# Half-wide operations where the second layer runs alone, and its input parts made a slot later

## The chip, the cores and the metric

The kernel runs on one core of one Trainium2 chip. The metric is the device time of an execution in microseconds. The engines are named as the profile names them: PE (TensorE, matrix products), PEld (its weight loads), DVE (VectorE), ACT (ScalarE), POOL (GpSimd) and SP (SyncE, which here only issues transfers).

## The reference

An attention with pooled keys feeds two layers in a row, each a product, a pointwise function and a second product. All tensors are float32, there are 12288 tokens of width 128, and each layer has 2048 hidden columns.

```
kv_pool = kv averaged over 4 x 4 patches          # 768 keys of width 128
k = v = kv_pool @ w_sr
a = softmax(q @ k.T / sqrt(128));  x1 = a @ v

h = x1 @ w_in1;  g = h * clip(h + 3, 0, 6) / 6;  x2 = g @ w_out1
h = x2 @ w_in2;  g = h if h >= 1, 0 if h <= -1, else (h + 1)^2 / 4
out = g @ w_out2
```

## The kernel before, in words

**Work and staging.** Tokens go in 24 blocks (`NB`) of 512, hidden columns in 8 pairs of 128 (`NPAIR`), so a layer has 192 steps `s` (`NS`): step s is pair s mod 8 of block s // 8. A float32 product is made as three products of a high and a low part (high by high, high weight by low input, low weight by high input). So `m_in(m, s)` (L461) is six products of 512 columns, three into each of two PSUM banks that form one tile `h` of 128x1024; two such tiles are in use, taken in turn. `m_out(m, s)` (L473) is six products that add into the one bank `acc[m]`, over the 8 steps of a block. m is 0 for the first layer and 1 for the second.

**Between the products** of the second layer a step goes through four engines' queues: `clip2` (L530, DVE, from the bank), `sq2` (L539, ACT), `max2` (L543, DVE, which is the last to read the bank), then `hi_lo` (L548): the high part is a copy on ACT (L555), the low part a subtraction on POOL (L556), on DVE only where s is 191. The first layer has `relu1` (L518, ACT), `mul1` (L523, DVE) and `hi_lo`. All of them work on 128x1024 at once, except where `parts` (L510) gives two halves of 128x512: from slot 20 on that is only s = 191 of either layer.

**Order.** The program is written out by hand: each engine runs its instructions in the order in which the loop over slots T (L743) issues them. Slot T takes step T of the first layer and step T - 11 (`O2`) of the second. Slots 0 to 19 are `early_slot` (L612), where a step has two separate banks; the others are `slot` (L650). There PE's order is `m_in(0, T)`, `m_out(1, ..)` by `out2` (L606), `m_in(1, T - 11)`, products of the attention in some slots, `m_out(0, T - 1)`. `out2` takes the step that is 13 slots behind, from slot 197 on 14 behind, so slot 197 has no `m_out(1, ..)`. From T = 192 on the first layer has nothing left but `m_out(0, 191)`, and the second layer runs alone, to slot 205; the same function `slot` issues that with conditions on T:

```
m_in(1, s2); clip2(s2); sq2(s2)
max2(s2 - 1); hi_lo(1, s2 - 1)
m_out(0, 191)        # slot 192 alone
out2(T)
```

**The input of the second layer.** When `m_out(0, s)` has ended a block, which is at the end of each slot T with T mod 8 = 0, it issues two instructions that make the high part `x2h` (L493, ACT) and the low part `x2l` (L494, DVE) from `acc[0]`. They are first needed three slots later, by `m_in(1, ..)`; `acc[0]` is written again by the `m_out(0, ..)` at the end of the next slot.

Of the kernel before, what the change touches and what calls it, by code (L numbers as in the profile page):

```python
# [9 lines left out]
F32R = mybir.dt.float32r  # L10
# [5 lines left out]
ALU = mybir.AluOpType  # L16
# [3 lines left out]
O2, LAG2 = 11, 2  # L20
# [20 lines left out]
JOIN_T = 20  # L41
# [5 lines left out]
def tile_attn_moe_moe2(  # L47
# [14 lines left out]
    nc = tc.nc  # L62
# [3 lines left out]
    BLK = 512  # L66
# [39 lines left out]
    def f32(t):  # L106
        return t.bitcast(FP32)
# [288 lines left out]
    def s_exp(b, j):  # L396
        e, su, s, ps, nm = e_t[b, j]
        if j == 3:
            qT_t.pop(b)
        if s is None:  # L400
            s2 = sm_p.tile([128, 2], FP32, tag="s2", name="s2")
            for h in range(2):
                nc.scalar.activation(
                    out=e[:, h * 384:(h + 1) * 384], in_=ps[h], func=ACTF.Exp, bias=nm, scale=1.0,
                    accum_out=s2[:, h:h + 1],
                )
            nc.vector.tensor_tensor(out=su, in0=s2[:, 0:1], in1=s2[:, 1:2], op=ALU.add)
        else:
            nc.scalar.activation(
                out=e.rearrange("p (a b) -> p a b", a=2), in_=s[:, :, :384], func=ACTF.Exp, bias=nm,  # L410
                scale=1.0, accum_out=su,
            )
# [48 lines left out]
    def m_in(m, s):  # L461
        b, c = divmod(s, NPAIR)
        assert (m, "in", c // 2) in ready
        hi, lo = (x_t, x2_t)[m][b]
        wh, wl = w_in[m]
        h_t[m, s] = new_pair() if paired(m, s) else [new_h(), new_h()]
        for k in range(2):
            ps = h_t[m, s][:, k] if paired(m, s) else h_t[m, s][k]
            ws = slice((2 * c + k) * 128, (2 * c + k + 1) * 128)
            for n, (l, r) in enumerate(((wh, hi), (wh, lo), (wl, hi))):  # L470
                nc.tensor.matmul(ps, l[:, ws], r, start=(n == 0), stop=(n == 2))  # L471

    def m_out(m, s):  # L473
        b, c = divmod(s, NPAIR)
        assert (m, "out", c // 2) in ready
        if c == 0:
            acc[m] = ps_a.tile([128, BLK], FP32, tag=f"acc{m}", name=f"acc{m}")
        hi, lo = hl_t.pop((m, s))
        wh, wl = w_out[m]
        order = [(k, n) for k in range(2) for n in range(3)]  # L480
        if (m, s) == (1, NS - 1):
            order = [(0, 0), (0, 2), (1, 0), (1, 2), (0, 1), (1, 1)]
        for i, (k, n) in enumerate(order):
            ws = slice((2 * c + k) * 128, (2 * c + k + 1) * 128)
            l, r = ((wh, hi), (wh, lo), (wl, hi))[n]
            nc.tensor.matmul(  # L486
                acc[m], l[:, ws], r[:, k, :], start=(c == 0 and i == 0), stop=(c == NPAIR - 1 and i == 5)
            )
        if c == NPAIR - 1:
            if m == 0:  # L490
                hi = x_p.tile([128, BLK], F32R, tag="x2h", name="x2h")
                lo = x_p.tile([128, BLK], F32R, tag="x2l", name="x2l")
                nc.scalar.copy(out=hi, in_=acc[0])  # L493
                nc.vector.tensor_tensor(out=lo, in0=acc[0], in1=f32(hi), op=ALU.subtract)  # L494
                x2_t[b] = (hi, lo)
            else:
                o_t[b] = acc[1]

    def o_T(b):
        o = o_p.tile([128, BLK], FP32, tag="o", name="o")  # L500
# [9 lines left out]
    def parts(m, s, h=None):  # L510
        h = h if h is not None else g_t[m, s]
        if not paired(m, s):
            return [(k, h[k] if isinstance(h, list) else h[:, k]) for k in range(2)]
        if s == NS - 1:
            return [(k, h[:, k]) for k in range(2)]
        return [(slice(0, 2), h)]

# [45 lines left out]
    def ok(s):  # L563
        return 0 <= s < NS
# [47 lines left out]
    def early_slot(T):  # L612
        s1, s2 = T, T - O2
        if ok(s1):
            m_in(0, s1)
            relu1(s1)
        if T in tail_at:
            s_tail_a(*tail_at[T], on_act=T < ACT_T)
        mul1(s1)
        if ok(s2):  # L620
            m_in(1, s2)
            clip2(s2)
        if ok(s2 - 1):
            hi_lo(1, s2 - 1)
        hi_lo(0, s1)
        if ok(s2):
            sq2(s2)
        if T in s_at:
            s_mm(*s_at[T])
        if T in tail_at:  # L630
            s_tail_b(*tail_at[T])
        if ok(s2):
            max2(s2)
        if T in s_at:
            s_exp(*s_at[T])
        if T in av_at:
            av(*av_at[T], early=T < O2)
        if T in q_at:
            q_T(q_at[T])
        conv_step(T in CONV_AT)  # L640
        load_next()
        if ok(s1 - 1):
            m_out(0, s1 - 1)
        if T in o_at:
            o_T(o_at[T])
        out2(T)
# [2 lines left out]

    def slot(T):  # L650
        s1, s2 = T, T - O2
        if ok(s1):
            m_in(0, s1)
        if ok(s2 - 1) and JOIN_T < T < NS:
            max2(s2 - 1)
        if T in tail_at and T > JOIN_T:
            s_exp(*tail_at[T])
        if ok(s1):
            relu1(s1)
        if ok(s2 - 1) and T < NS:  # L660
            hi_lo(1, s2 - 1)
        if T in tail_at:
            s_tail_a(*tail_at[T])
        if T < NS:
            out2(T)
        if ok(s1):
            mul1(s1)
        if T in o_at and T < NS:
            o_T(o_at[T])
        if ok(s2):  # L670
            m_in(1, s2)
        if ok(s1):
            hi_lo(0, s1)
        if ok(s2):
            clip2(s2)
        if ok(s2):
            sq2(s2)
        if ok(s2 - 1) and T >= NS:
            max2(s2 - 1)
            hi_lo(1, s2 - 1)  # L680
        if T in tail_at:
            s_tail_b(*tail_at[T])
        if T in s_at:
            s_mm(*s_at[T])
        if T in av_at:
            av(*av_at[T])
        if T in q_at:
            q_T(q_at[T])
        if ok(s1 - 1):
            m_out(0, s1 - 1)  # L690
        if T >= NS:
            out2(T)
            if T in o_at:
                o_T(o_at[T])

    with tc.manual_schedule():
        load_next()
        nc.scalar.dma_start(out=wsr, in_=w_sr)
        make_identity(nc, ident)
        nc.vector.tensor_reduce(  # L700
            out=pool_m.rearrange("p (a q) -> p a q", a=4),
            in_=ident.rearrange("p (a r q) -> p a q r", a=4, r=4), axis=AX.X, op=ALU.add,
        )
        nc.vector.tensor_scalar(out=pool_m, in0=pool_m, scalar1=1.0 / 16.0, scalar2=None, op0=ALU.mult)
        mem = {}

        def v_stat():
            mem["mxa"] = v_scale()

        def v_sv():  # L710
            mem["sv"] = v_split(mem["mxa"])

        def q_step(b):
            q_T(b)
            q_done.add(b)

        steps = {f"k{i}": (lambda i=i: kv_pool(i)) for i in range(NG // 2)}
        steps |= {f"g{i}": (lambda i=i: kv_sum_mm(i)) for i in range(NG // 2)}
        for m in range(KC):
            steps[f"t{m}"] = lambda m=m: kv_poolT(m)  # L720
            steps[f"p{m}"] = lambda m=m: k_mm(m)
            steps[f"z{m}"] = lambda m=m: k_split(m)
            steps[f"y{m}"] = lambda m=m: v_max(m)
        for n in range(len(w_jobs)):
            for st in range(4):
                steps[f"j{n}.{st}"] = lambda n=n, st=st: conv_stage(n, st)
        for j in range(4):
            steps[f"s{j}"] = lambda j=j: s_mm0(0, j, j in SPLIT0)
            steps[f"S{j}"] = lambda j=j: s_half(0, j, 1)
            steps[f"n{j}"] = lambda j=j: s_max(0, j, 0)  # L730
            steps[f"N{j}"] = lambda j=j: s_max(0, j, 1)
            steps[f"e{j}"] = lambda j=j: s_exp(0, j)
            steps[f"a{j}"] = lambda j=j: s_tail_a(0, j, True)
            steps[f"b{j}"] = lambda j=j: s_tail_b(0, j)
        steps |= {
            "vm": v_stat, "vs": v_sv, "vh": lambda: v_hi(mem["sv"]), "vl": lambda: v_lo(mem["sv"]),
            "q0": lambda: q_step(0), "q1": lambda: q_step(1),
            "x0": lambda: av(0, 0, True), "x1": lambda: av(0, 1, True),
        }
        for name in PROLOGUE.split():  # L740
            steps[name]()
            load_next()
        for T in range(NS + O2 + 16):  # L743
            if T == JOIN_T:
                join_banks()
            (early_slot if T < JOIN_T else slot)(T)


# [28 lines left out]
```

## Time and profile before

| what | value |
|---|---|
| median of 3 runs | 1387.58 us (1385.89 to 1390.67) |
| the profiled execution, its own time | 1386.09 us |
| its span, first to last instruction | 1384.3 us |
| PE busy | 1322.7 us, 96% of the span |
| DVE busy | 1104.6 us, 80% |
| POOL busy | 1057.2 us, 76% |
| ACT busy | 968.3 us, 70% |

The 1.8 us between the span and the profiled execution's time lie outside the first and last instruction. Busy shares are means over stages that differ: the first 200 us (keys, weights, early slots), a long middle, and the end from slot 192 on.

### The profile page before, as it was taken

What the parts mean: (1) busy time and instruction counts of PE and PEld (TensorE: products, weight loads), DVE (VectorE), ACT (ScalarE), POOL (GpSimd) and SP (SyncE); (2) the same over time, 40 slices, a digit from 0 to 9 for tenths busy, and PEclk for the clock granted to TensorE, in tenths of its full rate; (3) what the DMA queues carried; (4) which work ended last, traced back from release to release, by engine and by line L of the source; (5) the groups of instructions that cost most, each with busy time, mean ns of one, the idle gap of its engine ahead of it and who ended that gap; (6) DMA issues with size and microseconds to landing.
All of it is one profiled execution on the core that took longest, in us unless ns stands there. A gap on an engine that the chain in (4) does not pass through costs nothing.

```text
span 1384.3 us, 17050 instructions
## 1 busy us (share of the span) xinstructions
PE 1322.7 (96%) x6244; PEld 1070.6 (77%) x6244; DVE 1104.6 (80%) x1286; ACT 968.3 (70%) x1205; POOL 1057.2 (76%) x473
## 2 busy tenths in 40 slices
PE   8587999999999999999999999999999999999975
PEld 7465778888888888888888888888888888888754
DVE  3798978887887887888888888888878878877665
ACT  2677877767776776776777677677677767766753
POOL 2488988887887877787787787788877878778854
PEclk9799999999999999999999999999999999999999
DMA  9542121221221221221221212212212211211000
GB/s 320 135 83 50 46 50 31 42 43 35 46 38 35 39 50 35 39 50 27 47 42 31 50 31 42 51 31 42 45 34 45 39 35 31 42 35 20 8 3 14
DMA packets 260772, 66.20 MB, mean 48 GB/s; under 512 B 252368, under 2 KB 256592, under 8 KB 260688
## 3 DMA queue, kind: packets, MB, share of 16 engines
q1 hardware_dynamic: 259456, 62.94, 22.8%
q10 hardware_dynamic: 1232, 2.16, 0.4%
q8 instruction: 50, 0.82, 0.2%
q14 instruction: 34, 0.28, 0.1%
HBM read 21.04 MB, written 6.29 MB: 20 GB/s over the span
## 4 chain that ended last, share of the span: by engine, by line
PE 83%; DVE 7%; ACT 2%; POOL 2%; issue 2%; DMA 0%; POOLq 0%; DVEq 0%; ACTq 0%
PE h L471 36%; PE acc L486 35%; PE s L373 6%; PE s L445 6%; POOL l L556 1%; DVE g L535 1%; DVE g L546 1%; DVE a L430 1%; ACT h L555 1%; DVE t L526 1%; DVE nm L384 1%; DVE wa L181 0%; ACT t L521 0%; DVE t L535 0%; DVE t L546 0%
## 5 line engine op out<-in xcount | busy, mean ns | idle before, releaser
L556 POOL TENSOR_TENSOR l<-g,h 128x1024 fp32r<-128x1024 f32 (+1 forms) x195 | 451.0, 2315 | 249.4 <-issue 200.3
L556 POOL TENSOR_TENSOR l<-t,h 128x1024 fp32r<-128x1024 f32 (+1 forms) x216 | 540.8, 2507 | 20.9 <-ACT h L555 15.2
L526 DVE SCALAR_TENSOR_TENSOR t<-t,h 128x1024 f32<-128x1024 f32 (+1 forms) x213 | 235.1, 1111 | 94.0 <-ACT t L521 93.7
L521 ACT ACTIVATE t<-h 128x1024 f32<-128x1024 f32 (+1 forms) x213 | 198.9, 942 | 135.9 <-PE h L471 90.7
L535 DVE TENSOR_SCALAR g<-h 128x1024 f32<-128x1024 f32 (+1 forms) x195 | 227.8, 1172 | 67.7 <-PE h L471 65.0
L541 ACT ACTIVATE g<-g 128x1024 f32<-128x1024 f32 (+1 forms) x195 | 198.4, 1021 | 114.9 <-DVE g L535 111.7
L555 ACT CAST h<-t 128x1024 fp32r<-128x1024 f32 (+1 forms) x220 | 210.7, 965 | 84.9 <-DVE t L526 82.8
L546 DVE TENSOR_TENSOR g<-h,g 128x1024 f32<-128x1024 f32 (+1 forms) x195 | 226.2, 1164 | 21.2 <-ACT g L541 21.1
L555 ACT CAST h<-g 128x1024 fp32r<-128x1024 f32 (+1 forms) x195 | 194.9, 1005 | 6.1 <-DVE g L546 5.4
L471 PE MATMUL h<-x2h,wi1h 128*128 128x512 f32 x384 | 155.1, 404 | 12.8 <-DVE g L546 6.8
L471 PE MATMUL h<-xh,wi0h 128*128 128x512 f32 x384 | 152.9, 398 | 7.7 <-ACT xh L450 5.0
L486 PE MATMUL acc<-l,wo1h 128*128 128x512 f32 x384 | 152.1, 397 | 8.3 <-POOL l L556 8.3
L486 PE MATMUL acc<-h,wo0h 128*128 128x512 f32 x384 | 156.3, 407 | 0.0
L486 PE MATMUL acc<-l,wo0h 128*128 128x512 f32 x384 | 153.1, 399 | 2.3 <-POOL l L556 2.1
L471 PE MATMUL h<-xl,wi0h 128*128 128x512 f32 x384 | 152.5, 397 | 0.7 <-DVE xl L451 0.7
L471 PE MATMUL h<-x2h,wi1l 128*128 128x512 f32 x384 | 152.2, 396 | 0.0
L486 PE MATMUL acc<-h,wo0l 128*128 128x512 f32 x384 | 152.2, 396 | 0.0
L471 PE MATMUL h<-xh,wi0l 128*128 128x512 f32 x384 | 152.1, 396 | 0.0
L486 PE MATMUL acc<-h,wo1h 128*128 128x512 f32 x384 | 151.6, 395 | 0.3 <-ACT h L555 0.3
L471 PE MATMUL h<-x2l,wi1h 128*128 128x512 f32 x384 | 151.7, 395 | 0.0
L486 PE MATMUL acc<-h,wo1l 128*128 128x512 f32 x384 | 151.4, 394 | 0.0
L430 DVE SCALAR_TENSOR_TENSOR a<-e,rc,a 128x768 f16<-128x768 f32 x96 | 133.5, 1390 | 0.6 <-ACT a L423 0.5
(136 smaller groups left out, 2122.2 us busy)
## 6 DMA issues: line engine op xcount, KB each, us to landing
q<-in_q_dram SPq DMA_DIRECT2D x96, 64.0 KB, 2.3
out_dram<-o SPq DMA_DIRECT2D x96, 64.0 KB, 1.9
h<-in_kv_dram SPq DMA_DIRECT2D x4, 512.0 KB, 8.8
l<-in_moe_w_in_dram SPq DMA_DIRECT2D x3, 512.0 KB, 9.1
at<-a SPq DMA_TRANSPOSE x96, 3.7
g<-in_moe_w_in_dram SPq DMA_DIRECT2D x2, 512.0 KB, 6.6
h<-in_moe_w_out_dram SPq DMA_DIRECT2D x2, 512.0 KB, 9.3
l<-in_kv_dram ACTq DMA_DIRECT2D x2, 512.0 KB, 10.5
```

The lines of the kernel that those rows point to most:

```text
L373: nc.tensor.matmul(ps[h], l[:, js], r[:, ks], start=(n == 0), stop=(n == 2))
L430: nc.vector.scalar_tensor_tensor(out=a[:, 1], in0=e, scalar=rc, in1=a[:, 0], op0=ALU.mult, op1=ALU.subtract)
L445: nc.tensor.matmul(ps, l[:, k, :], r[:, k, :], start=(n == 0), stop=(n == 3 * KC - 1))
L471: nc.tensor.matmul(ps, l[:, ws], r, start=(n == 0), stop=(n == 2))
L486: nc.tensor.matmul(acc[m], l[:, ws], r[:, k, :], start=(c == 0 and i == 0), stop=(c == NPAIR - 1 and i == 5))
L521: nc.scalar.activation(out=g[:, p], in_=h, func=ACTF.Relu, scale=1.0 / 6.0, bias=0.5)
L526: nc.vector.scalar_tensor_tensor(out=g[:, p], in0=g[:, p], scalar=1.0, in1=h, op0=ALU.min, op1=ALU.mult)
L535: nc.vector.tensor_scalar(out=g[:, p], in0=h, scalar1=1.0, scalar2=-1.0, op0=ALU.min, op1=ALU.max)
L541: nc.scalar.activation(out=g, in_=g, func=ACTF.Square, scale=0.5, bias=0.5)
L546: nc.vector.tensor_tensor(out=g[:, p], in0=h, in1=g[:, p], op=ALU.max)
L555: nc.scalar.copy(out=hi[:, p], in_=g)
L556: eng.tensor_tensor(out=lo[:, p], in0=g, in1=f32(hi[:, p]), op=ALU.subtract)
```

## The change

The two instructions that make `x2h` and `x2l` leave `m_out` and become a function `x2_parts`. In early slots it stands where it stood. In `slot(T)` it is called with T - 1, behind `mul1` of slot T: so the parts of a block are made in the slot after the one that ended the block, on ACT behind `relu1` and the copy of `hi_lo(1, ..)`, on DVE behind `max2`, the start of a softmax tail and `mul1`. For the last block it comes in slot 193.

The slots from 192 on get a function of their own, `last_slot`. In it `max2(s2)` follows `sq2(s2)` in the same slot, `hi_lo(1, s2 - 1)` stands between `clip2(s2)` and `sq2(s2)`, and `max2` of step 180 comes first of all. `parts` now gives two halves for the second layer's steps 181 to 191, which are those that `last_slot` starts, so `clip2`, `sq2`, `max2` and `hi_lo` of these steps are two half-wide instructions each. The products, their order on PE and the lag of `out2` are the same. The conditions that fall out of `slot` change nothing in its order.

```
--- before.py
+++ after.py
@@ -486,15 +486,19 @@
             nc.tensor.matmul(
                 acc[m], l[:, ws], r[:, k, :], start=(c == 0 and i == 0), stop=(c == NPAIR - 1 and i == 5)
             )
-        if c == NPAIR - 1:
-            if m == 0:
-                hi = x_p.tile([128, BLK], F32R, tag="x2h", name="x2h")
-                lo = x_p.tile([128, BLK], F32R, tag="x2l", name="x2l")
-                nc.scalar.copy(out=hi, in_=acc[0])
-                nc.vector.tensor_tensor(out=lo, in0=acc[0], in1=f32(hi), op=ALU.subtract)
-                x2_t[b] = (hi, lo)
-            else:
-                o_t[b] = acc[1]
+        if c == NPAIR - 1 and m == 1:
+            o_t[b] = acc[1]
+
+
+    def x2_parts(t):
+        b, c = divmod(t - 1, NPAIR)
+        if t < 1 or c != NPAIR - 1:
+            return
+        hi = x_p.tile([128, BLK], F32R, tag="x2h", name="x2h")
+        lo = x_p.tile([128, BLK], F32R, tag="x2l", name="x2l")
+        nc.scalar.copy(out=hi, in_=acc[0])
+        nc.vector.tensor_tensor(out=lo, in0=acc[0], in1=f32(hi), op=ALU.subtract)
+        x2_t[b] = (hi, lo)
 
     def o_T(b):
         o = o_p.tile([128, BLK], FP32, tag="o", name="o")
@@ -511,7 +515,7 @@
         h = h if h is not None else g_t[m, s]
         if not paired(m, s):
             return [(k, h[k] if isinstance(h, list) else h[:, k]) for k in range(2)]
-        if s == NS - 1:
+        if s >= NS - (O2 if m else 1):
             return [(k, h[:, k]) for k in range(2)]
         return [(slice(0, 2), h)]
 
@@ -641,6 +645,7 @@
         load_next()
         if ok(s1 - 1):
             m_out(0, s1 - 1)
+            x2_parts(T)
         if T in o_at:
             o_T(o_at[T])
         out2(T)
@@ -649,35 +654,24 @@
 
     def slot(T):
         s1, s2 = T, T - O2
-        if ok(s1):
-            m_in(0, s1)
-        if ok(s2 - 1) and JOIN_T < T < NS:
+        m_in(0, s1)
+        if T > JOIN_T:
             max2(s2 - 1)
-        if T in tail_at and T > JOIN_T:
-            s_exp(*tail_at[T])
-        if ok(s1):
-            relu1(s1)
-        if ok(s2 - 1) and T < NS:
-            hi_lo(1, s2 - 1)
+            if T in tail_at:
+                s_exp(*tail_at[T])
+        relu1(s1)
+        hi_lo(1, s2 - 1)
         if T in tail_at:
             s_tail_a(*tail_at[T])
-        if T < NS:
-            out2(T)
-        if ok(s1):
-            mul1(s1)
-        if T in o_at and T < NS:
+        out2(T)
+        mul1(s1)
+        x2_parts(T - 1)
+        if T in o_at:
             o_T(o_at[T])
-        if ok(s2):
-            m_in(1, s2)
-        if ok(s1):
-            hi_lo(0, s1)
-        if ok(s2):
-            clip2(s2)
-        if ok(s2):
-            sq2(s2)
-        if ok(s2 - 1) and T >= NS:
-            max2(s2 - 1)
-            hi_lo(1, s2 - 1)
+        m_in(1, s2)
+        hi_lo(0, s1)
+        clip2(s2)
+        sq2(s2)
         if T in tail_at:
             s_tail_b(*tail_at[T])
         if T in s_at:
@@ -686,12 +680,27 @@
             av(*av_at[T])
         if T in q_at:
             q_T(q_at[T])
-        if ok(s1 - 1):
-            m_out(0, s1 - 1)
-        if T >= NS:
-            out2(T)
-            if T in o_at:
-                o_T(o_at[T])
+        m_out(0, s1 - 1)
+
+    def last_slot(T):
+        s2 = T - O2
+        if T == NS:
+            max2(s2 - 1)
+        if ok(s2):
+            m_in(1, s2)
+            clip2(s2)
+        if ok(s2 - 1):
+            hi_lo(1, s2 - 1)
+        if ok(s2):
+            sq2(s2)
+            max2(s2)
+        if T == NS:
+            m_out(0, NS - 1)
+        if T == NS + 1:
+            x2_parts(NS)
+        out2(T)
+        if T in o_at:
+            o_T(o_at[T])
 
     with tc.manual_schedule():
         load_next()
@@ -743,7 +752,7 @@
         for T in range(NS + O2 + 16):
             if T == JOIN_T:
                 join_banks()
-            (early_slot if T < JOIN_T else slot)(T)
+            (early_slot if T < JOIN_T else slot if T < NS else last_slot)(T)
 
 
 # ---- launch: one core; inputs and outputs as the reference has them ----
```

## Rows read from the trace of the kernel before

**Rows 1.** Busy time by stretch: stretch, its length, then busy us (x instructions) of each engine.

```profile
1327.80:1378.97 51.17, 34.03 (x133) 23.89 (x132) 30.32 (x28) 24.78 (x26) 26.17 (x11) 1.00 0.03 6
...
100.00:1320.00 1220.00, 1208.81 (x5693) 982.25 (x5694) 999.63 (x1136) 883.57 (x1063) 980.31 (x423) 1.00 0.21 39
```

**Rows 2.** Waits from 200 to 1320 us: engine, line, releaser, total us, times, longest.

```profile
PE h L471 <- DVE g L546: 1.1, 2, 0.7
```

**Rows 3.** Waits from 1327 us to the end, the three that held PE.

```profile
PE acc L486 <- POOL l L556: 8.3, 6, 2.0
...
PE h L471 <- DVE t L546: 5.0, 3, 2.6
PE h L471 <- DVE g L546: 3.5, 3, 1.2
```

**Rows 4.** PE in order of time, end: start us, us, engine, line, out<-in [idle before <-releaser].

```profile
1329.06 0.47 PE L471 MATMUL h<-x2h,wi1h 128*128 128x512 f32 x1 [1.04 <-DVE g L546]
...
1332.61 0.50 PE L486 MATMUL acc<-l,wo1h 128*128 128x512 f32 x1 [1.70 <-POOL l L556]
...
1338.41 0.40 PE L471 MATMUL h<-x2h,wi1h 128*128 128x512 f32 x1
...
1355.69 0.47 PE L471 MATMUL h<-x2h,wi1h 128*128 128x512 f32 x1 [1.20 <-DVE g L546]
...
1359.93 0.47 PE L471 MATMUL h<-x2h,wi1h 128*128 128x512 f32 x1 [1.21 <-DVE t L546]
...
1368.42 0.47 PE L471 MATMUL h<-x2h,wi1h 128*128 128x512 f32 x1 [1.21 <-DVE t L546]
...
1369.90 0.40 PE L486 MATMUL acc<-h,wo1h 128*128 128x512 f32 x1
...
1371.28 0.40 PE L486 MATMUL acc<-h,wo1h 128*128 128x512 f32 x1
...
1378.47 0.63 PE L486 MATMUL acc<-l,wo1h 128*128 128x512 f32 x2
```

**Rows 5.** DVE in order of time, end of the span.

```profile
1327.68 1.23 DVE L546 TENSOR_TENSOR g<-h,g 128x1024 f32<-128x1024 f32 x1
...
1357.43 1.22 DVE L535 TENSOR_SCALAR g<-h 128x1024 f32<-128x1024 f32 x1 [1.89 <-PE h L471]
1358.57 1.21 DVE L546 TENSOR_TENSOR t<-h,t 128x1024 f32<-128x1024 f32 x1
...
1370.17 1.29 DVE L535 TENSOR_SCALAR t<-h 128x512 f32<-128x512 f32 x2 [1.89 <-PE h L471]
...
1374.28 3.09 DVE L556 TENSOR_TENSOR l<-t,h 128x512 fp32r<-128x512 f32 x2 [0.49 <-ACT h L555]
```

**Rows 6.** ACT in order of time, end of the span.

```profile
1370.89 1.23 ACT L541 ACTIVATE t<-t 128x512 f32<-128x512 f32 x2 [1.48 <-DVE t L535]
...
1373.63 1.13 ACT L555 CAST h<-t 128x512 fp32r<-128x512 f32 x2
```

**Rows 7.** POOL in order of time, from 110 to 185 us: half-wide subtractions.

```profile
118.88 3.36 POOL L556 TENSOR_TENSOR l<-t,h 128x512 fp32r<-128x512 f32 x2 [1.10 <-ACT h L555]
...
138.18 2.55 POOL L556 TENSOR_TENSOR l<-g,h 128x512 fp32r<-128x512 f32 x2
```

**Rows 8.** POOL in order of time, end of the span.

```profile
1330.19 2.37 POOL L556 TENSOR_TENSOR l<-g,h 128x1024 fp32r<-128x1024 f32 x1 [5.92 <-ACT h L555]
```

**Rows 9.** All engines in order of time, from 380 to 393 us, slot 49.

```profile
382.96 0.69 DVE L494 TENSOR_TENSOR x2l<-acc,x2h 128x512 fp32r<-128x512 f32 x1 [0.90 <-ACT x2h L493]
...
384.81 1.06 ACT L555 CAST h<-g 128x1024 fp32r<-128x1024 f32 x1
...
388.30 0.48 PE L486 MATMUL acc<-h,wo0h 128*128 128x512 f32 x1
```

**Rows 10.** DVE and PE in order of time, from 1284 to 1288 us, slot 185.

```profile
1285.21 0.69 DVE L494 TENSOR_TENSOR x2l<-acc,x2h 128x512 fp32r<-128x512 f32 x1 [1.60 <-ACT x2h L493]
...
1287.18 0.47 PE L471 MATMUL h<-x2h,wi1h 128*128 128x512 f32 x1 [0.70 <-DVE g L546]
```

## The prediction

> **What bounds the kernel now.** I read first the busy time by stretch [rows 1]. From 100 to 1320 us PE is busy for 1208.81 of 1220 us, so nothing that another engine does faster can show there. From 1327.80 to 1378.97, where the second layer runs alone, it is busy for 34.03 of 51.17 us, and DVE, ACT and POOL are less busy still: no engine is the bound there, so a chain of handovers must be. The waits agree. From 200 to 1320 us PE waited 1.1 us for `max2` in all [rows 2]; at the end it waited 8.3 + 5.0 + 3.5 = 16.8 us, for POOL's low parts and for `max2` [rows 3].
>
> The order of time shows the chain. From slot 199 on the first product of a step starts every 4.24 us (1355.69, 1359.93), each time released by DVE [rows 4]. In between, `clip2` starts at 1357.43, when all six products are done, `max2` **of the step before** follows it at 1358.57 and ends at 1359.78, and 0.15 later PE may start [rows 5]. So the bank of step s is given back only after the `clip2` of step s + 1, and PE, whose twelve products take far less, waits. In slots 193 to 196 the same lateness goes on to the copy on ACT and the subtraction on POOL, and `m_out` waits for that (1332.61, after 1.70 us) [rows 4]; the pitch is about 4.45 there.
>
> **The end, part by part.** First the prices. Six products take 1371.28 - 1369.90 = 1.38 us [rows 4], so 0.23 each, and the twelve of a slot 2.8 us. On DVE a whole operation lasts 1.22, but the next starts 1.14 after it (1357.43, 1358.57); two halves last 1.29 together [rows 5]. With the same overlap a half holds DVE for 0.61 and has its result after 0.69. On ACT two halves of the copy last 1.13, and the two of `sq2` 1.23, the second waiting for its `clip2` [rows 6]: 0.52 to 0.6 each, result after 0.63. On POOL two halves last 2.55 where nothing else delays them and 3.36 in the worst row [rows 7], against 2.37 for a whole [rows 8]. I take 2.55, since POOL's whole subtractions at the end are the short ones too. The price of halving is thus 0.07 us per pair on DVE and 0.18 on POOL; it buys that the next engine starts after half an operation. That halves are handed on one by one is seen at step 191: `sq2` starts at 1370.89, when DVE's pair (1370.17, 1.29 long) is half done [rows 5, 6]. `clip2`, though, starts only after all six products even there, so I give it no earlier start.
>
> Now one slot in the new order. DVE does `clip2` of s in two halves (0 and 0.61), ACT's first half of `sq2` runs from 0.78 to 1.41, DVE goes on with `max2` of the **same** step at 1.45 and 2.06, and is free at 2.67. ACT's `hi_lo` copy of s - 1 lies ahead of `sq2` and fits into the 0.78. Per slot that asks 2.67 of DVE, 2.55 of POOL, about 2.3 of ACT and 2.8 of PE. PE sets the pitch, by little, and a bank is given back a whole slot before it is wanted.
>
> I carried this on as a recurrence: each engine takes its queue in order, each instruction starts when its engine is free and its inputs are there, plus the gaps seen between engines (0.04 to 0.15 us). Run on the order of before, it ends at 1378.8, where the trace has 1378.47 + 0.63 = 1379.1 [rows 4]. On the new order:
> - Slot 192 gains nothing. `max2` of step 180 is whole and comes after its `sq2` as before (1327.68 [rows 5]), so step 182 starts at 1329.06 as before, and POOL's subtraction for step 180 (1330.19, 2.37 long [rows 8]) releases `m_out` as before.
> - Step 184 starts at 1336.6 instead of 1338.41 [rows 4]: the low part of step 181 is ready at 1335.1, not 1337.1.
> - Steps 185 to 190 start at 1339.4, 1342.2, 1344.5, 1347.8, 1350.6 and 1353.4, so 2.8 apart but for slot 197, which has no `m_out` of the second layer.
> - Step 191 starts at 1356.2 instead of 1368.42 [rows 4]. Its own chain then ends the kernel: `clip2` at 1358.2 (DVE still has `max2` of 190), `max2` done at 1361.0, the two low parts on DVE from 1361.2, 3.09 long as before [rows 5], so 1364.3, and the last product ends at 1364.7.
>
> Model against model that is 1378.8 - 1364.7 = **14.1 us** less. `o_T` and the output transfers behind it are the same.
>
> **The input parts.** This moves two instructions and adds none; no DMA moves, SP's and POOL's queues are not passed. Before, in the slot that follows a block, `x2l` stands first on DVE, waits 0.90 for ACT (slot 49), and only then may `max2` start [rows 9]; PE, which has slack there, does not wait. Once it did: in slot 185, which has no attention products, `max2` stood behind `x2l` (1285.21) and PE waited 0.70 us [rows 10]. That wait goes.
>
> New in slot 49: ACT reaches `x2h` after the copy that starts at 384.81 and lasts 1.06 [rows 9], so 385.9 to 386.5; DVE has done `mul1` by 386.1 and makes `x2l` from 386.5 to 387.15. Behind it `clip2`, the softmax tail and the next slot's `max2` come 0.4 us later, and that `max2` has over a microsecond in hand. `acc[0]` is wanted by PE at 388.30 [rows 9]: 1.1 us in hand, because 2 us of attention products stand ahead. This holds for the 20 slots of this kind; in slot 185 it does not. There `x2l` would end at about 1288.4, and PE would come to `m_out(0, 184)` at 1287.7: a wait of 0.7 to 0.8, which is what the other wait gave back. I count the move as 0 in all, with 1 us to either side.
>
> **Sum.** From the profiled execution's own time: 1386.09 - 14.1 = 1372.0. It stands 1.5 us below the median of the runs shown (1387.58); the changed kernel will be timed as that median is, so I forecast 1387.58 - 14.1 = **1373.5 us**, 1.0% less.
>
> **Rivals.**
> 1. *Halves cost more, and another engine becomes the bound.* If every POOL pair took 3.36 us as in the worst row [rows 7], the low parts would come 3.3 apart and the same recurrence gives a gain of 10.5, so 1377.1; DVE halves of 0.72 instead of 0.61 give 12.4. For it: DVE asks 2.67 of 2.8, little room. Against: 3.36 is from a stretch with weight conversion and attention beside it, which the end hasn't. [...] Chance 0.17.
> 2. *PE alone is the bound.* With no wait after step 184 the 18 groups of six that are left from 1336.6 take 18 x 1.39 = 25.0, and the last ends at 1361.8: a gain of 17.3, 1370.3. Against: the last step's two subtractions on DVE. Chance 0.07.
> 3. *The halves are not handed on singly*, each consumer waiting for both, as `clip2` does for its six products. Then DVE idles through both halves of `sq2`; the recurrence gives a gain of 1.9, 1385.7, which is no change. Against it stands the start of `sq2` above. Chance 0.06.
> 4. *Slower: `acc[0]` is held too long.* If `x2l` ended more than 1.1 us later than I work out, PE would wait in each of 20 slots at `m_out(0, ..)`, 2.0 us in all for each further 0.1. To eat the gain and 4.2 us more it must be 0.9 beyond, so 2.0 late in every block; 2.2 late gives 22 - 14.1, so 1395.5. For it: x2 now stands behind `relu1`, a copy and `mul1`, which wait for PE. Against: all of these have their times in the trace. Chance 0.04.
>
> **How the numbers follow.** The forecast (a gain of 12.5 to 15.5) has 0.66. A measurement of this kernel tells 0.3%, 4.2 us, from no change. Faster is the forecast with rivals 1 and 2, 0.90; within 0.3% is rival 3, 0.06; slower is rival 4, 0.04. The range runs from 1370.0 (rival 2) to 1379.5 (rival 1 with the runs' own spread, some 2 us above); rivals 3 and 4 stay out.
>
> **What would show it.** In the profile after: first products of steps 184 to 191 about 2.8 apart; PE's waits from 1327 us on at 5 us or less instead of 16.8, most of it before step 184 and in the last step; pairs on DVE of 1.29 and on POOL of 2.55; `max2` of a step before the `clip2` of the next; up to slot 184 the same times as now within 1 us, and `m_out(0, ..)` waiting for `x2l` in slot 185 alone. I am wrong if the pitch is above 3.2, if POOL's pairs take 3 us, or if PE waits for `x2l` in every eighth slot.

## The result, and the profile after

Four runs of the changed kernel against four of the kernel before: median 1366.67 us (1364.92 to 1372.9) against 1387.49, ratio 0.9855 with the 95% interval 0.9818 to 0.9892. The change makes the kernel faster by 1.45%. Forecast were 1373.5 us and a range down to 1370.0: the sign was right, and so was the mechanism, but the forecast gain of 14.1 us was 7 us too small, and the time lies outside the range.

The profiled execution took 1372.9 us, the longest of the four; what made it long comes further down. It is therefore read by stretches. A second profile of each kernel was taken in the experiments, and the table holds both:

| stretch | before | before again | after | after again |
|---|---|---|---|---|
| start to the first product of slot 20, us | 189.51 | 187.88 | 192.29 | 186.20 |
| from there to the first product of step 181 | 1134.14 | 1134.08 | 1134.25 | 1132.26 |
| from there to the end of the span | 60.65 | 61.64 | 44.16 | 44.24 |

The first profile after is long in its run-in, where PE stood still for 5.98 us. Slots 20 to 22, right behind that, take 1.7 us more there: up to 195.8 us PE's products are 0.43 us apart instead of 0.23, at a granted clock of 0.50 (192.2 to 195.5 us) against 0.98 from 195.8 to 199. Without that its middle is as short as the second's. The end, where the forecast put all of the gain, lost 16.5 us (60.65 to 44.16). The waits from 1327 us to the end, in the kernel after, against [rows 3]:

```profile
PE acc L486 <- POOL l L560: 1.7, 1, 1.7
...
PE h L471 <- DVE g L550: 1.0, 1, 1.0
...
PEld h L471 <- DVE g L550: 0.6, 1, 0.6
PEld h L471 <- DVE t L550: 0.5, 1, 0.5
```

Of 16.8 us of waiting on PE 2.7 are left, and both waits are of the first slots, as the order of time on PE shows. The rows answer to [rows 4]; here the first product of step 181 is at 1326.54, so 2.89 us later than before.

```profile
1331.95 0.47 PE L471 MATMUL h<-x2h,wi1h 128*128 128x512 f32 x1 [1.04 <-DVE g L550]
...
1335.50 0.50 PE L486 MATMUL acc<-l,wo1h 128*128 128x512 f32 x1 [1.68 <-POOL l L560]
...
1339.55 0.41 PE L471 MATMUL h<-x2h,wi1h 128*128 128x512 f32 x1
...
1342.34 0.39 PE L471 MATMUL h<-x2h,wi1h 128*128 128x512 f32 x1
...
1345.14 0.39 PE L471 MATMUL h<-x2h,wi1h 128*128 128x512 f32 x1
...
1346.75 0.50 PE L471 MATMUL h<-x2h,wi1h 128*128 128x512 f32 x1
...
1349.94 0.50 PE L471 MATMUL h<-x2h,wi1h 128*128 128x512 f32 x1
...
1358.41 0.39 PE L471 MATMUL h<-x2h,wi1h 128*128 128x512 f32 x1
...
1364.92 0.62 PE L486 MATMUL acc<-l,wo1h 128*128 128x512 f32 x2
```

By this list only step 182 waits for its bank; steps 184, 185 and 186 are 2.8 apart, the twelve products' own time. Steps 187 and 188 (1346.75, 1349.94) wait for theirs too, which shows in the rows of the weight loads alone: these waited 0.5 and 0.6 us for `max2`, and the two steps begin 0.2 and 0.3 us later than the product ahead of them would let them. Step 191 begins 31.9 us after step 181, where it was 44.8 (1368.42 - 1323.65).

DVE, ACT and POOL in the steady part and at the last step, against [rows 5, 6, 8]:

```profile
1352.39 1.28 DVE L539 TENSOR_SCALAR g<-h 128x512 f32<-128x512 f32 x2
...
1352.66 2.57 POOL L560 TENSOR_TENSOR l<-t,h 128x512 fp32r<-128x512 f32 x2
...
1353.10 1.23 ACT L545 ACTIVATE g<-g 128x512 f32<-128x512 f32 x2
...
1353.77 1.29 DVE L550 TENSOR_TENSOR g<-h,g 128x512 f32<-128x512 f32 x2
```

```profile
1354.97 1.28 DVE L539 TENSOR_SCALAR t<-h 128x512 f32<-128x512 f32 x2
...
1360.42 2.56 POOL L560 TENSOR_TENSOR l<-g,h 128x512 fp32r<-128x512 f32 x2
...
1362.97 1.29 DVE L560 TENSOR_TENSOR l<-t,h 128x512 fp32r<-128x512 f32 x2
```

`clip2` in halves, `sq2` 0.71 behind it, `max2` of the same step at once behind `clip2`, and the next `clip2` 2.58 after the first: the loop of the forecast, priced there at 2.67. From slot 197 on, which has no `m_out(1, ..)`, DVE runs it almost without a pause. The pairs last 1.28 and 1.29 on DVE, 2.57 on POOL, as taken from rows 5 and 7. The last line is the one that differs: the two low parts of step 191 on DVE take 1.29 us, not 3.09.

### The profile page after: what moved, and what is told of

Its sections match the earlier page's. It is cut to its first block, busy times and chain, and to the rows that moved or that the text cites. A ratio compares the mean times of both kernels' runs of the same rounds, so it can differ in the third digit from the quotient of the medians.

```text
span 1370.7 us, 17088 instructions
## 1 busy us (share of the span) xinstructions
PE 1315.7 (96%) x6244; PEld 1070.4 (78%) x6244; DVE 1107.5 (81%) x1306; ACT 964.0 (70%) x1225; POOL 1058.3 (77%) x483
## 4 chain that ended last, share of the span: by engine, by line
PE 84%; DVE 6%; ACT 2%; POOL 2%; issue 1%; DMA 0%; ACTq 0%; DVEq 0%; POOLq 0%
PE h L471 36%; PE acc L486 36%; PE s L373 6%; PE s L445 6%; DVE a L430 1%; POOL l L560 1%; DVE t L530 1%; DVE nm L384 1%; ACT t L525 1%; DVE g L539 1%; DVE wa L181 1%; DVE g L550 1%; ACT h L559 0%; DVE wa L183 0%; DMA wst<-in_moe_w_out_dram 0%
## 5 line engine op out<-in xcount | busy, mean ns | idle before, releaser
L430 DVE SCALAR_TENSOR_TENSOR a<-e,rc,a 128x768 f16<-128x768 f32 x96 | 133.2, 1388 | 0.6 <-ACT a L423 0.5
```

What stands on the lines that cost most here:

```text
L430: nc.vector.scalar_tensor_tensor(out=a[:, 1], in0=e, scalar=rc, in1=a[:, 0], op0=ALU.mult, op1=ALU.subtract)
```

## The experiments

**1. The changed kernel again.** No edit; five runs.

> The changed kernel once more, unaltered, for a second profile and a firmer time. Measure: the end, from the first product of step 181 to the end of the span, is 60.65 us before (1384.3 - 1323.65) and 44.16 us in the first profile after (1370.7 - 1326.54). Theory A, all of the gain is in the end: the end is 44.2 again within 0.3, the time is 16.5 us under that of before in the mean of five rounds (ratio 0.988), and what differs more between executions arises before 200 us, where one DVE subtraction of the softmax tail took 6.35 us in the first profile: it takes under 2.2 us in a faster execution, and step 20 then waits 1.3 us and not 6. Theory B, the moved input parts save 4 us more in the middle: the time is 20 us under before (ratio 0.9855) and the stretch from slot 20 to step 181 is 4 us shorter than before.

Measured: median 1367.38 us against 1386.90, ratio 0.9849 (0.9822 to 0.9877). The end is 44.24. The middle, from slot 20 to step 181, is 1132.26, 1.9 us shorter than before. So theory A is right about the end and wrong about the middle, and theory B's 4 us are not there either. This execution (1364.52 us) has no long subtraction of a softmax tail, the longest is 2.15, and slot 20 waits 1.34.

**2. The end alone.** The functions for the last slots and the halves stay; the input parts go back.

```
-        if c == NPAIR - 1 and m == 1:
-            o_t[b] = acc[1]
+        if c == NPAIR - 1:
+            if m == 0:
+                hi = x_p.tile([128, BLK], F32R, tag="x2h", name="x2h")
+                lo = x_p.tile([128, BLK], F32R, tag="x2l", name="x2l")
+                nc.scalar.copy(out=hi, in_=acc[0])
+                nc.vector.tensor_tensor(out=lo, in0=acc[0], in1=f32(hi), op=ALU.subtract)
+                x2_t[b] = (hi, lo)
+            else:
+                o_t[b] = acc[1]
...
-        x2_parts(T - 1)
...
```

> The new order and the halves of the last slots, with the input parts made where they were before, right behind the products that end a block. Theory A: same time as the changed kernel within 1 us, end of 44.2 + at most 1, PE waits for max2 in slot 185 (0.7 us) as before. Theory B: 4 us slower than the changed kernel.

Measured: 1368.08 us, ratio 0.9850 (0.9821 to 0.9879); end 44.26, middle 1133.8, and PE waits 0.71 us for `max2` in slot 185. The end is all there without the moved parts. In the time the two kernels are 0.7 us apart, which the spread of the runs does not resolve.

**3. The moved parts alone.** `x2_parts` as in the change; the last slots in the old order, whole.

```
-        if s >= NS - (O2 if m else 1):
+        if s == NS - 1:
...
-        if T == NS:
-            max2(s2 - 1)
         if ok(s2):
             m_in(1, s2)
             clip2(s2)
+            sq2(s2)
         if ok(s2 - 1):
+            max2(s2 - 1)
             hi_lo(1, s2 - 1)
-        if ok(s2):
-            sq2(s2)
-            max2(s2)
```

> The moved input parts alone; last slots in the order of before, whole operations. Theory A: same as before within 1 us, end 60.6 with at most 1 us to either side, since only the last block's parts lie in it; in slot 185 PE waits 0.5 us for x2l in place of 0.7 for max2. Theory B: 4 us faster than before.

Measured: 1384.12 us against 1386.90, ratio 0.9976 (0.9956 to 0.9996); middle 1132.36, end 61.81. The move is worth 1.7 us in the middle, between the two theories. The end is 0.2 us beyond what was expected; its last products ran at a lower granted clock (0.60 from 1373.0 to 1377.2 us), of which experiment 9 tells more. Slot 185 is as expected: PE waits 0.53 for `x2l` (the prediction had 0.7 to 0.8) in place of 0.70 for `max2` [rows 10], so it is not the source of more than 0.2 us.

The source is in the 20 slots for which the prediction had no wait. `max2`, and PE's weight loads and products behind it, in slot 49, before:

```profile
383.56 1.21 DVE L546 TENSOR_TENSOR g<-h,g 128x1024 f32<-128x1024 f32 x1
```

```profile
384.47 0.19 PEld L486 LDWEIGHTS acc<-h,wo1l 128*128 128x128 f32 x1
384.89 0.19 PEld L471 LDWEIGHTS h<-x2h,wi1h 128*128 128x128 f32 x1 [0.23 <-PE acc L486]
```

```profile
384.70 0.40 PE L486 MATMUL acc<-h,wo1l 128*128 128x512 f32 x1
384.94 0.46 PE L471 MATMUL h<-x2h,wi1h 128*128 128x512 f32 x1
385.23 0.39 PE L471 MATMUL h<-x2l,wi1h 128*128 128x512 f32 x1
```

and in the second profile after:

```profile
381.18 0.39 PE L486 MATMUL acc<-h,wo1l 128*128 128x512 f32 x1
381.18 0.19 PEld L471 LDWEIGHTS h<-x2h,wi1h 128*128 128x128 f32 x1
...
381.41 0.39 PE L471 MATMUL h<-x2h,wi1h 128*128 128x512 f32 x1
...
381.64 0.40 PE L471 MATMUL h<-x2l,wi1h 128*128 128x512 f32 x1
```

Before, `max2` stood behind `x2l` and ended at 383.56 + 1.21 = 384.77. The load of the next weights had to wait for the bank, and came at 384.89 after 0.23 us, only 0.05 ahead of its product. (The row names the product ahead as the releaser; that it was DVE's order is shown by experiment 4.) The product started 0.24 behind the last (no idle time that the list of PE's waits would show), and the one behind it 0.29 later instead of 0.23. After, the load lies 0.23 ahead of its product and all starts are 0.23 apart. That is 0.07 us a block, 1.4 in the 20 blocks and most of the 1.7. The waits of the weight loads from 200 to 1270 us count the blocks, before and in the second profile after:

```profile
PEld h L471 <- PE acc L486: 13.8, 40, 0.8
```

```profile
PEld h L471 <- PE acc L486: 8.8, 20, 0.8
```

**4. Only the low part moved.** In the changed kernel the high part `x2h` is made on ACT where it was before.

```
+        if c == NPAIR - 1 and m == 0:
+            hi = x_p.tile([128, BLK], F32R, tag="x2h", name="x2h")
+            nc.scalar.copy(out=hi, in_=acc[0])
+            x2_t[b] = hi
...
-        hi = x_p.tile([128, BLK], F32R, tag="x2h", name="x2h")
+        hi = x2_t[b]
```

> The changed kernel, but the high part x2h is made where it was before (ACT, behind the products that end a block); only the low part x2l on DVE comes behind mul1 of the next slot. Measure: the first product of slot 25 to that of slot 185, 1060.9 us before, 1059.1 in the second profile after. Theory A, the 1.6 us come of max2 no longer standing behind x2l on DVE, so that PE loads the next weights in time in each of the 20 slots: 1059.2 again. Rival, they come of ACT's queue being freed: 1060.8.

Measured: from slot 25 to slot 185 it takes 1059.02 us (1280.37 - 221.35); the end is 44.21. The 20 waits of the weight loads are gone here too. ACT's order for `x2h` is that of before, so DVE's queue alone made the loss, theory A. This is a single execution, so its time of 1366.09 us settles nothing beside that.

**5. The order without the halves.** Last slots in the new order, with whole operations but for step 191; input parts as before.

```
-        if s >= NS - (O2 if m else 1):
+        if s == NS - 1:
...
```

The part that is not shown puts the input parts back, as in experiment 2.

> The new order of the last slots with whole operations (step 191 alone in halves, as before), input parts as before. My recurrence gives 5.7 us of gain, end about 55; a chain clip2, sq2, max2 of whole operations is 3.5 us long per step, against a pitch of 4.2 before. A rival, that the order alone brings it and halves only shorten the last chain: a gain of 12 us or more.

Measured: 1377.36 us, ratio 0.9920 (0.9896 to 0.9943); end 53.09, a gain of 7.6. The last steps come 3.48 apart, and DVE shows why:

```profile
1355.30 1.23 DVE L557 TENSOR_TENSOR g<-h,g 128x1024 f32<-128x1024 f32 x1 [1.13 <-ACT g L552]
1356.44 1.22 DVE L546 TENSOR_SCALAR t<-h 128x1024 f32<-128x1024 f32 x1
1358.79 1.23 DVE L557 TENSOR_TENSOR t<-h,t 128x1024 f32<-128x1024 f32 x1 [1.13 <-ACT t L552]
...
1366.63 1.67 DVE L567 TENSOR_TENSOR l<-t,h 128x512 fp32r<-128x512 f32 x2
```

Between `clip2` (1356.44) and `max2` of the same step (1358.79) DVE stands idle for 1.13 us while ACT makes the whole `sq2`: from start to start 1.22 + 1.06 + the handovers = 2.35. The rival (12 us from the order alone) falls. The recurrence gave 5.7, 1.9 too little. It had the last low parts at 3.09, and they take 1.67 here, but that explains little of it: PE starts its last two products at 1369.41, 1.1 us after these low parts are done, so with 3.09 the end would come some 0.2 us later, an estimate. The rest of the 1.9 is open.

**6. The halves without the order.** The kernel before with only the rule for halves changed.

```
-        if s == NS - 1:
+        if s >= NS - (O2 if m else 1):
```

> The kernel before with the halves alone: steps 181 to 191 in two halves, the order of before. The recurrence gives a gain of 1.1 us, end 59.5, since max2 still stands behind the next step's clip2 and PE waits for it; a rival, that halves bring most of the gain: an end under 52.

Measured: end 61.06; step 191 begins 44.85 after step 181, as before (44.77), so the pitch gains nothing. PE still waits for `max2` (1.25 us before 1359.98, 1.24 before 1364.29), which stands behind both halves of the next `clip2`. The end is no shorter than the 60.65 of before, but the last eight products ran at a granted clock of 0.55, and start some 0.43 apart.

```profile
1371.70:1375.30 3.60, 3.54 (x8) 2.28 (x8) 0.55 (x1) 0.00 (x0) 0.01 (x1) 0.55 0.00 0
```

At 0.23 apart they would end 1.4 us sooner, which gives 59.6, an estimate, and is what the recurrence had. So neither part makes the gain alone: about 1 for the halves, 7.6 for the order, 16.4 together.

**7. POOL reads beside DVE's last low parts.** Two subtractions are added on POOL in slot 203; their result is used nowhere.

```
+        if T == NS + O2:
+            junk = x_p.tile([128, BLK], F32R, tag="x2l", name="x2l")
+            for k in range(2):
+                nc.gpsimd.tensor_tensor(out=junk, in0=f32(w_in[0][0])[:, k * 512:k * 512 + 512], in1=f32(w_in[0][1])[:, k * 512:k * 512 + 512], op=ALU.subtract)
```

> The changed kernel, with two half-wide subtractions of weight parts added on POOL in slot 203, into a buffer that nothing reads; they start when POOL has done step 190, which is when DVE starts the two last low parts. Theory A, DVE's subtraction of two SBUF operands stands still while POOL reads SBUF: the pair of DVE goes from 1.29 us back to 2.3 or more (3.09 in the kernel before), the end from 44.2 to over 45. Rival: the 3.09 came of something else in the kernel before (its last step's order); then the pair stays at 1.29 and the end at 44.2.

DVE and POOL at the last step:

```profile
1357.84 3.50 DVE L560 TENSOR_TENSOR l<-t,h 128x512 fp32r<-128x512 f32 x2
```

```profile
1357.80 2.98 POOL L690 TENSOR_TENSOR x2l<-wi0h,wi0l 128x512 fp32r<-128x512 f32 x2
```

**8. POOL writes there, and reads nothing.** Fills in the same place.

```
+        if T == NS + O2:
+            junk = x_p.tile([128, BLK], F32R, tag="x2l", name="x2l")
+            for k in range(2):
+                nc.gpsimd.memset(f32(junk), 0.0)
```

> The same with two fills (memset) of the same size on POOL in place of the subtractions, so POOL writes SBUF and reads nothing. If only POOL's reading holds DVE up, the pair of DVE stays at 1.29; if any use of SBUF by POOL does, it is 1.9 or more.

```profile
1356.46 1.29 DVE L560 TENSOR_TENSOR l<-t,h 128x512 fp32r<-128x512 f32 x2
```

```profile
1356.40 1.12 POOL L690 MEMSET x2l<- 128x512 f32 x2
```

With POOL reading, DVE's pair takes 3.50 us and the end 45.71; with POOL filling a buffer it takes 1.29 and the end 44.26. The 3.09 of [rows 5], which began at 1374.28, was therefore 1.3 of work and 1.8 of delay beside POOL's subtraction of step 190, which in the kernel before ran to 1376.2:

```profile
1373.87 2.35 POOL L556 TENSOR_TENSOR l<-g,h 128x1024 fp32r<-128x1024 f32 x1 [1.91 <-ACT h L555]
```

Such pairs elsewhere agree: the longer POOL's subtraction still runs beside DVE's pair, the longer that pair takes, 1.67 us for 0.5 us beside each other (experiment 5), 1.77 for 0.6 (experiment 10), 3.09 for 1.9, 3.15 for 2.0 (step 191 of the first layer in the first profile after: DVE's pair starts at 1325.17, POOL's subtraction ends at 1327.17), and 3.50 for 2.9 (experiment 7).

**9. The kernel before again.** No edit, one execution.

> The kernel before, unaltered, for a second profile of it. The end is 60.65 again within 0.3, and slot 20 to step 181 1134.0 (first profile 1134.14). Open is the run-in, from the start to slot 20: 189.51 in the first profile, and 186.2 to 189.0 in the kernels with the change whose trace shows no long subtraction. If it is 187 to 189 here, the two kernels do not differ there and the change is worth 16.5 + 1.9 = 18.4 us; if 189.5 or more again, something of the change shortens the run-in too.

Measured: 187.88 to slot 20, in the span of the kernels with the change (186.2 to 189.0 in eight profiles without a long subtraction), so the run-in is not shown to differ. It varies as much without the change: 185.69 in experiment 6, 189.51 in the first profile. Middle 1134.08. The end is 61.64, not within 0.3 of 60.65, though step 191 begins 44.79 after step 181 in both. The last six or so products make the difference:

```profile
1375.88 0.40 PE L486 MATMUL acc<-h,wo1h 128*128 128x512 f32 x1
1376.12 0.59 PE L486 MATMUL acc<-h,wo1l 128*128 128x512 f32 x1
1376.50 0.63 PE L486 MATMUL acc<-h,wo1h 128*128 128x512 f32 x1
```

```profile
1374.50:1379.40 4.90, 3.81 (x11) 2.52 (x11) 1.92 (x3) 0.00 (x0) 0.05 (x1) 0.67 0.00 0
```

```profile
1376.20:1379.10 2.90, 2.82 (x11) 1.99 (x11) 1.17 (x2) 0.00 (x0) 0.02 (x1) 1.00 0.00 0
```

The first of the two windows is of this profile, the second of the first profile. From 1376.12 the products are 0.4 apart and not 0.23. The granted clock (the first figure behind the bracket of POOL) is 0.67 over the first window and 1.00 in the second. PE had been idle for 2.00 us before 1374.61, waiting for POOL; the first profile has the same wait, 2.00 us before 1376.27, and no such fall. The same is seen in the third experiment (granted 0.60 from 1373.0 to 1377.2) and the sixth (0.55 from 1371.7 to 1375.3), and in neither profile of the changed kernel, whose PE does not stop there (products 0.23 apart to the end in both; granted 1.00 from 1358 to 1366 us in the first). So the last products of the old order cost 1.0 to 1.4 us more in three of its four profiles, an estimate from their spacing; what lowers the clock was not tried, and how often it falls in other executions is not known.

**10. A better version: `clip2` ahead of the last low parts of the first layer.** The changed kernel, and in slot 191 `clip2` of step 180 in front of `hi_lo(0, 191)`.

```
         m_in(1, s2)
+        if T == NS - 1:
+            clip2(s2)
         hi_lo(0, s1)
-        clip2(s2)
+        if T < NS - 1:
+            clip2(s2)
         sq2(s2)
```

> The changed kernel with one thing more: in slot 191 clip2 of step 180 stands ahead of hi_lo(0, 191) on DVE, not behind its two low parts (3.15 us). Then max2 of step 180 is done some 2 us earlier, the wait of 1.04 us before step 182 goes and that of 1.70 for POOL's low part shrinks to about 0.9, with perhaps 0.3 at m_out(0, 191): the end is 42.4, not 44.2. In the time that is 1.8 us, 0.13%, which rounds can hardly tell. Rival: the low parts of step 191 come too late for m_out(0, 191) and the end stays at 44 or more.

Measured: 1364.27 us against 1385.45, ratio 0.9847 (0.9819 to 0.9875); end 41.87, 2.3 us less than the changed kernel's. The wait before step 182 is gone, and the one for POOL is this:

```profile
1325.97 0.50 PE L486 MATMUL acc<-l,wo1h 128*128 128x512 f32 x1 [0.65 <-POOL l L560]
```

The low parts on DVE took less as well, since they now start when POOL has almost done with its own:

```profile
1318.20 1.23 DVE L539 TENSOR_SCALAR g<-h 128x1024 f32<-128x1024 f32 x1 [0.34 <-PE h L471]
1319.34 1.77 DVE L560 TENSOR_TENSOR l<-t,h 128x512 fp32r<-128x512 f32 x2
```

1.77 us in place of 3.15; the end came 0.5 sooner than expected. It beats both kernels by the trace; against the changed kernel the times (1364.27 and 1367.38, from different sets of runs) only agree with that.

## Why the prediction was right, and where it failed

**The mechanism held.** The chain named as the bound, a bank given back only behind the next step's `clip2`, is gone, and but for steps 187 and 188 PE sets the pitch: 2.79 for 2.8. Slot 192 gained nothing (step 182 begins 5.41 us behind step 181 in both kernels, with the same waits of 1.04 and 1.7), step 184 begins 13.0 behind (forecast 1336.6 - 1323.65 = 12.95), and step 191 31.9 (32.55). The halving costs what the rows had: 0.07 on DVE, 0.2 on POOL. Rivals 1 and 3 are refuted by the pairs of 1.29 and 2.57 and by `sq2` starting 0.71 behind `clip2`; rival 4, a bank held too long, by the middle, which got shorter; rival 2 came nearest, with the end 16.5 shorter against its 17.3. It is nearly what happened: from the start of step 184 to the end of the last product PE needs 26.0 us (1339.55 to 1365.54) where the rival had 25.2, and the late starts of steps 187 and 188 are 0.5 of it. (Its 17.3 counts from the trace's 1379.1; from the recurrence's 1378.8, as the 14.1 does, it is 17.0.)

**Where it fell short.** The sum had 14.1. By the traces the change is worth 16.4 at the end and 1.8 in the middle, 18.2 us, or 1 us and more beyond that where the old end ran at the lower clock. Three terms failed.
- "the two low parts on DVE from 1361.2, 3.09 long as before": they take 1.29. The price came from a row in which POOL ran beside DVE, and in the new order it does not: POOL's last pair ends at 1362.98, and DVE's begins at 1362.97. Experiments 7 and 8 show the cause. Of the 1.8 us 1.4 reach the end: the forecast had 8.5 us from the start of step 191 to the end of the last product (1356.2 to 1364.7), and the trace has 7.1 (1358.41 to 1365.54), in which PE runs 30 products without a stop and is the bound itself. With 2.2 us put back onto the pair, in experiment 7, the end grew by 1.5.
- "PE, which has slack there, does not wait" and "I count the move as 0": it was worth 1.7 to 1.9. With it failed the premise, "nothing that another engine does faster can show there", read from a busy time of 1208.81 of 1220 us: a product that takes longer because its weights come late counts as busy all the while (0.46 for 0.40 us in slot 49). PE's list of waits had nothing; the loss was a late weight load and showed in the rows of PEld. Experiments 3 and 4 show it. The sign "up to slot 184 the same times as now within 1 us" failed with this term.
- "2.67" per slot on DVE: it is 2.58. Step 191 begins 0.65 sooner behind step 181 than forecast, and that arises at step 187, which waits for DVE: it comes 1.61 behind step 186 where the forecast had 2.3. That the 0.09 a slot make up all of it is not shown.

The 0.3 that is then missing at the end lies in the recurrence itself, which had the old order end at 1378.8 and not 1379.1.

**The rest of the 7 us**, 1 to 3 us, stays open; the lower clock of the old end may be part of it. The medians of the two comparisons differ by 20.8 and 19.5 us; the interval of the second comparison, 0.9822 to 0.9877, is 17 to 25 us, and holds the 18 to 19 of the traces. The range was too tight at its lower end: it allowed the best case at the end, PE alone as the bound, and nothing for the middle.

## What to carry to other kernels

When a step's result is wanted by another engine only so that a buffer comes free, order it before the next step's first operation, and make the operations short enough that the same engine isn't idle between the two; either alone brought less than half here (7.6 and about 1 of 16.4 us). A duration from a trace holds for the neighbours that it ran beside (the same pair took 3.09 us here and 1.29): look whether they are still there in the new order. On an engine that is never idle, look at the weight loads' waits too: a product that starts on time can still be slow (0.46 us for 0.40 here).

## What was not expected of the hardware

In the first profile after, one subtraction of a softmax tail (`s_tail_b`, L430, two operands in SBUF) took 6.35 us on DVE, where the others take 1.0 to 2.2, and PE waited 5.98 us at slot 20 in place of 1.3. DVE, POOL and PE there:

```profile
184.59 6.35 DVE L430 SCALAR_TENSOR_TENSOR a<-e,rc,a 128x768 f16<-128x768 f32 x1
```

```profile
183.92 1.30 POOL L349 TENSOR_TENSOR ql<-qT,qh 128x512 fp32r<-128x512 f32 x1
185.18 2.51 POOL L560 TENSOR_TENSOR l<-g,h 128x512 fp32r<-128x512 f32 x2
187.65 2.48 POOL L560 TENSOR_TENSOR l<-t,h 128x512 fp32r<-128x512 f32 x2
```

```profile
192.29 0.76 PE L471 MATMUL h<-xh,wi0h 128*128 128x512 f32 x1 [5.98 <-DVE g L550]
```

POOL went through five subtractions without a gap, to 190.13, and DVE ended 0.8 us behind the last. In the kernel before, at the same place, it was the other way round:

```profile
186.45 1.45 DVE L430 SCALAR_TENSOR_TENSOR a<-e,rc,a 128x768 f16<-128x768 f32 x1
```

```profile
187.05 3.23 POOL L556 TENSOR_TENSOR l<-g,h 128x512 fp32r<-128x512 f32 x2
```

DVE took 1.45 and POOL's pair 3.23 instead of 2.55. Which of the two is delayed was decided otherwise in this one of twelve profiles, for the same instructions; what decides it was not tried. PE's wait at slot 20 grew by 4.6 us with it, and this execution was about 5 us longer than the next longest of its four. No difference between the kernels rests on it.
